# A rewritten order list for a fused attention and gated MLP kernel: four operations change their places in the queues, and two things derived from the list change with it

## The chip, the cores and the metric

The kernel runs on one core of a Trainium2 chip. A time is the device time of one launch in microseconds (us); of several runs the median is given. The core has TensorE (PE: matmuls, and PEld for its weight loads), VectorE (DVE), ScalarE (ACT), GpSimd (POOL), and SyncE (SP), whose queue issues the DMA transfers.

## The reference

```python
def _attn_ref(q, k, v):                       # (4, 12, 448, 64) each
    scores = (1 / np.sqrt(64)) * np.matmul(q, k.transpose(0, 1, 3, 2))
    scores = np.where(mask, -1e9, scores)     # mask: above the diagonal
    scores = scores - np.max(scores, axis=-1, keepdims=True)
    attn = np.exp(scores)
    attn = attn / (np.sum(attn, axis=-1, keepdims=True) + 1e-09)
    return np.matmul(attn, v)

def _moe_ref(x, w_in, w_spatial, b_spatial, w_out):
    h = np.maximum(x @ w_in, 0.0)             # x: (4, 448, 768), the heads side by side
    u, v = h[..., :512], h[..., 512:]
    v_n = (v - mean(v)) / np.sqrt(var(v) + 1e-06)
    v_s = np.einsum('ts,bsd->btd', w_spatial, v_n) + b_spatial[None, :, None]
    return (u * v_s) @ w_out                  # (4, 448, 768)
```

## The kernel before

The work is written as a plan of 2496 operations, numbered in the order in which the functions of the kernel add them. An operation (`plan.add`) is one or a few instructions of one engine, with the tiles that it reads and writes. The heads are taken in 24 pairs (`p`; four batches of six pairs), and each batch goes through the gated MLP (`ffn`) once its pairs are done.

- `load(p)` (L701, L708) fetches q and k of a pair; the early pairs in four loads of 112 KB, one per head. `v_load` (L876) fetches v, `prep_in` (L1324) a piece of `w_in`.
- `qk_turn(p)` turns q and k with transposes on PE (L738, L764) and copies them out of PSUM (L747, L749, L785, L787); for the later pairs a DMA transpose does it and DVE or POOL copies it `across` (L847).
- `wide(p)` serves the early pairs: scores (L934), row maximum on DVE (L972), exponential on ACT (L982), sums (L993, L1001), scaling (L487 to L491), PE transposes (L1021), copies (L1045, L1047). `attend(p)` serves the others: scores (L1101, L1102), mask and maximum (L1112), exponential (L1124), weights (L1213), and for all pairs the product with v (L1255). `gram` (L583) and `total` (L604) are PE work for scale factors.
- `ffn(b)` has, for each of four tiles of rows (`t`, 128 rows and at the end 64), a chain of matmuls (L1473) into a PSUM bank `pf`, ReLU on ACT into a buffer `hv` (L1536), statistics (L1544 to L1570, with a power on POOL at L1563), the normalisation (L1580, L1582, L487) and the low half of the result into `vn` (L1595, on DVE or POOL). Then follow `u`, the product with `w_spatial`, and the output. `hv` has two buffers for the four tiles.

Engines are set by a string `WHERE`, and the order by hand, in the list `ORDER` (from L57), one sequence of all 2496 numbers. `Plan.run` (L237) walks the list once and puts each operation at the end of its engine's queue. So only the order of two operations of one engine reaches the chip. But two more things are taken from the walk.

*Buffers.* A buffer is given to an operation's tile at the tile's first use in the list, from the front of a line of free ones, and returns to the end of that line at its last use in the list. The operation then waits for all that used the buffer before:

```python
if b.slot is None:
    b.slot, b.before = free[b.kind].pop(0)
    left[b] = len(b.ops)
waits += b.before
```

*Fillers.* The walk keeps a clock of its own for every engine (`busy`), made of costs written in the source. DVE work and POOL work that stand next to each other in the list exclude each other in this clock (`pool_end`, `dve_end`). While the clock of PE is under `WARM = 46000` (ns), and PE would have to wait for the next operation by this clock, it puts filler matmuls into PE's queue, `self.warm` (L689: ones times ones, 128 x 128 by 256 columns of f16, into PSUM bank 2 of `pf`, read by nobody):

```python
while now + (fill := FILL if now > 6000 else 2 * FILL) < start - 40:
    order.append((self.warm, e))
    now += fill
```

The clock is used for nothing else: at run time the filler stands in PE's queue as any matmul.

Of the kernel before, what the change touches and what calls it, by code (L numbers as in the profile page):

```python
# [56 lines left out]
    10, 1, 5, 0, 3, 73, 8, 6, 72, 100, 2, 75, 74, 4, 9, 14, 12, 11, 15, 96, 13, 26, 97, 22, 98, 93, 7, 16, 148, 18,  # L57
    17, 92, 99, 149, 20, 19, 95, 101, 21, 102, 106, 107, 103, 110, 108, 111, 104, 109, 76, 114, 113, 105, 116, 112,
    115, 27, 120, 118, 117, 157, 28, 119, 94, 121, 164, 126, 132, 160, 158, 165, 127, 122, 161, 166, 78, 23, 167,
    123, 168, 162, 79, 139, 159, 163, 124, 170, 136, 169, 77, 125, 172, 142, 137, 171, 256, 138, 131, 173, 140, 176,  # L60
    29, 152, 141, 143, 177, 257, 153, 30, 190, 128, 193, 150, 174, 133, 178, 24, 154, 151, 130, 129, 144, 175, 156,
    155, 194, 181, 135, 134, 25, 261, 195, 186, 179, 185, 34, 180, 191, 260, 196, 264, 80, 187, 265, 192, 84, 82,
    268, 188, 31, 189, 83, 267, 269, 262, 266, 32, 270, 197, 272, 271, 274, 263, 273, 33, 275, 258, 276, 38, 198,
    182, 81, 35, 259, 46, 278, 36, 184, 277, 315, 279, 280, 37, 183, 316, 318, 285, 42, 282, 253, 283, 284, 319,
    145, 314, 290, 281, 252, 328, 321, 294, 306, 322, 320, 326, 300, 297, 307, 323, 329, 254, 39, 317, 255, 325, 40,
    327, 295, 330, 85, 296, 41, 324, 298, 289, 86, 286, 43, 331, 503, 301, 44, 287, 397, 291, 288, 332, 302, 87, 45,
    202, 310, 88, 334, 402, 47, 333, 311, 89, 500, 338, 90, 336, 335, 146, 206, 351, 398, 48, 293, 147, 344, 348,
    309, 49, 312, 339, 50, 395, 51, 199, 52, 399, 308, 60, 57, 299, 394, 63, 66, 313, 58, 61, 292, 403, 200, 59, 54,
    502, 404, 201, 64, 396, 55, 337, 62, 406, 303, 414, 354, 416, 415, 56, 410, 67, 407, 411, 417, 405, 343, 510,
    409, 207, 412, 572, 208, 501, 413, 509, 203, 587, 69, 422, 423, 507, 418, 573, 304, 439, 588, 419, 204, 408,  # L70
    440, 209, 349, 441, 420, 520, 210, 421, 305, 350, 427, 522, 497, 521, 340, 65, 523, 426, 355, 342, 431, 53, 345,
    341, 356, 352, 424, 205, 400, 70, 428, 425, 346, 524, 68, 214, 401, 589, 347, 498, 353, 429, 506, 496, 430, 525,
    71, 508, 505, 526, 499, 532, 528, 436, 504, 725, 533, 357, 442, 529, 534, 538, 531, 432, 536, 535, 956, 211,
    539, 212, 443, 530, 437, 358, 542, 213, 433, 537, 574, 543, 215, 222, 444, 435, 549, 527, 359, 434, 438, 544,
    216, 734, 511, 91, 545, 540, 513, 445, 561, 737, 548, 541, 738, 558, 512, 741, 217, 739, 562, 546, 742, 554,
    218, 559, 563, 547, 514, 553, 590, 560, 446, 564, 729, 570, 740, 447, 733, 731, 730, 555, 223, 1030, 732, 591,
    557, 743, 224, 728, 550, 556, 744, 726, 565, 225, 552, 515, 727, 566, 551, 735, 1029, 516, 1052, 517, 518, 519,
    955, 567, 751, 219, 907, 745, 977, 747, 746, 752, 220, 748, 736, 908, 1293, 753, 757, 788, 749, 568, 221, 226,
    750, 569, 783, 1292, 785, 754, 795, 784, 770, 791, 592, 781, 796, 786, 762, 755, 227, 792, 779, 763, 593, 756,
    780, 787, 758, 798, 789, 228, 782, 773, 594, 793, 1033, 797, 229, 767, 799, 575, 794, 1031, 230, 800, 231, 771,  # L80
    232, 805, 234, 764, 237, 759, 246, 602, 240, 235, 247, 238, 236, 617, 576, 241, 239, 243, 603, 242, 249, 577,
    806, 244, 362, 801, 363, 817, 604, 248, 360, 595, 766, 760, 361, 802, 364, 765, 618, 365, 761, 807, 250, 790,
    245, 772, 251, 816, 774, 370, 596, 808, 835, 368, 366, 978, 367, 837, 369, 1032, 605, 775, 597, 834, 371, 836,
    811, 606, 812, 833, 838, 818, 373, 824, 813, 598, 819, 820, 768, 599, 372, 803, 607, 769, 839, 600, 374, 814,
    375, 578, 815, 840, 821, 376, 804, 377, 378, 579, 383, 822, 387, 809, 847, 619, 381, 843, 385, 848, 620, 776,
    384, 887, 389, 823, 388, 849, 382, 1051, 850, 386, 841, 777, 810, 580, 390, 844, 641, 827, 888, 778, 825, 601,
    846, 642, 581, 851, 845, 1034, 889, 826, 233, 853, 828, 582, 608, 857, 890, 379, 391, 891, 1053, 583, 852, 893,
    894, 842, 895, 584, 892, 609, 829, 854, 896, 1054, 901, 910, 610, 1058, 1059, 855, 898, 392, 830, 917, 902,
    1055, 393, 856, 611, 903, 448, 899, 460, 913, 585, 612, 858, 911, 1057, 918, 831, 900, 613, 859, 861, 914, 643,
    614, 1060, 921, 644, 586, 904, 919, 862, 860, 832, 615, 655, 920, 616, 621, 915, 622, 864, 449, 876, 656, 869,  # L90
    450, 1291, 623, 877, 1065, 1294, 624, 645, 451, 916, 868, 1290, 646, 625, 879, 452, 870, 1295, 873, 1056, 453,
    626, 657, 1299, 380, 872, 878, 1301, 627, 905, 897, 658, 923, 922, 628, 906, 874, 571, 863, 461, 659, 924, 454,
    629, 462, 1066, 912, 1062, 630, 463, 865, 875, 1067, 484, 871, 660, 866, 1063, 929, 880, 867, 631, 925, 1064,
    980, 632, 927, 661, 992, 926, 633, 930, 634, 1068, 981, 993, 943, 982, 635, 647, 648, 455, 946, 931, 456, 886,
    636, 881, 928, 457, 464, 1004, 994, 939, 983, 1016, 490, 458, 465, 1005, 882, 995, 985, 1061, 1017, 984, 459,
    1069, 932, 996, 997, 986, 1006, 1070, 1018, 987, 998, 485, 637, 999, 1041, 486, 988, 1000, 638, 989, 1300, 487,
    1001, 639, 990, 1306, 466, 1019, 991, 488, 1039, 669, 979, 1007, 909, 1020, 491, 885, 670, 1003, 1021, 489, 944,
    1296, 1002, 933, 671, 1022, 1008, 949, 945, 672, 1010, 1009, 1024, 492, 640, 947, 950, 1011, 934, 493, 662, 948,
    467, 478, 938, 1012, 649, 468, 1013, 940, 1297, 1367, 469, 663, 1015, 883, 472, 470, 1014, 1315, 942, 1303, 951,
    884, 1023, 935, 471, 1304, 1316, 1327, 941, 1307, 1317, 1339, 1305, 937, 673, 494, 664, 1366, 1340, 650, 1308,  # L100
    1298, 1328, 1318, 1368, 1341, 665, 1319, 1369, 1329, 683, 495, 1342, 1370, 666, 684, 1309, 936, 1330, 1320,
    1314, 674, 1321, 1351, 1343, 1332, 1373, 1371, 473, 952, 1331, 1352, 675, 1377, 1322, 1365, 1333, 1374, 1345,
    1344, 1334, 1324, 479, 474, 1380, 685, 480, 1040, 1323, 1353, 1346, 475, 676, 1025, 481, 1335, 677, 1336, 1378,
    678, 1381, 1325, 1038, 1379, 1338, 651, 1348, 1364, 1354, 1337, 1347, 652, 1355, 1326, 953, 1382, 679, 1356,
    954, 653, 1310, 667, 1357, 1383, 1026, 668, 1349, 654, 1350, 958, 1311, 1358, 686, 1027, 680, 482, 1401, 957,
    476, 1028, 1389, 681, 483, 687, 959, 1042, 1413, 960, 961, 964, 682, 962, 1302, 697, 968, 965, 1390, 1414, 698,
    971, 1388, 969, 1415, 708, 1123, 972, 970, 709, 1360, 688, 973, 1425, 1416, 703, 1391, 689, 1035, 974, 699,
    1426, 1417, 704, 477, 966, 1392, 1419, 1418, 1402, 710, 1393, 1124, 1359, 1420, 1403, 700, 1384, 1421, 1394,
    1395, 1422, 711, 701, 1441, 705, 1396, 1424, 1397, 706, 1423, 1440, 1663, 692, 1398, 1439, 975, 693, 976, 1037,
    1664, 963, 1399, 1442, 967, 707, 1400, 1662, 1086, 712, 1098, 1404, 1087, 713, 1044, 694, 1088, 1665, 714, 1099,  # L110
    1089, 1443, 695, 1444, 1438, 1100, 1090, 1140, 1091, 1445, 1447, 1512, 1101, 1451, 1092, 1448, 1093, 715, 1094,
    1385, 1103, 696, 1095, 1452, 716, 1102, 1096, 717, 1453, 1097, 1036, 1104, 1372, 1446, 1110, 1105, 1107, 1454,
    1141, 1111, 1106, 1043, 1142, 1108, 1455, 1112, 1109, 1456, 1406, 1045, 1074, 1405, 1113, 1114, 719, 1075, 1115,
    1073, 1457, 1076, 1046, 1143, 1047, 1077, 1048, 1116, 720, 1078, 1049, 721, 1079, 1119, 1071, 1080, 722, 1081,
# [1646 lines left out]
```

## Time and profile before

| | |
|---|---|
| median of 3 runs | 358.98 us (358.64, 358.98, 359.28) |
| span of the profiled execution | 358.6 us |
| PE busy | 346.2 us, 97% |
| PEld busy | 225.5 us, 63% |
| DVE busy | 285.9 us, 80% |
| ACT busy | 268.7 us, 75% |
| POOL busy | 161.6 us, 45% |
| mean granted TensorE clock | 0.998 of full speed |

The span runs from the first to the last instruction of the one profiled execution; the time of a run holds what lies around that too. For the profiled execution the page gives the span alone. A timeline row is a run of like instructions: its start, its length from the first start to the last end, how many, and the idle time of the engine before it with what ended that. Ends of matmuls are modelled: rows that follow each other on PE overlap.

### The profile page before, as it was taken

How to read it: one execution, taken by the hardware profiler on the slowest of the kernel's cores; microseconds unless marked ns; L12 is line 12 of the kernel's file. 1: busy time of each engine (PE TensorE's matmuls, PEld its weight loads, DVE VectorE, ACT ScalarE, POOL GpSimd, SP SyncE). 2: the span in 40 equal slices, each digit the busy share in tenths (PEclk: the TensorE clock that was granted, in tenths of full speed). 3: DMA queues.
4: the chain of work that ended last, by engine and by line, in shares of the span. 5: the costliest groups of instructions: out<-in, count | busy, mean ns of one | idle time of the engine just before them, and what ended most of it. 6: DMA issues, size and time to landing. Idle time of an engine off the chain costs nothing.

```text
span 358.6 us, 8098 instructions
## 1 busy us (share of the span) xinstructions
PE 346.2 (97%) x2602; PEld 225.5 (63%) x2602; DVE 285.9 (80%) x1116; ACT 268.7 (75%) x767; POOL 161.6 (45%) x223
## 2 busy tenths in 40 slices
PE   6999899999999999999999999999999999999995
PEld 5476555665555556765455579755755885555695
DVE  4899889999999999889898998987989994263420
ACT  3698899999999999888799989748789684231101
POOL 3133664337656468364374572334686710042400
PEclk9999999999999999999999999999999999999999
DMA  7959979746768999999997898997767978300014
GB/s 162 210 164 242 244 170 215 174 100 166 150 166 186 208 237 181 178 182 139 188 180 153 172 225 162 205 174 156 164 116 156 159 111 174 82 2 0 3 47 130
DMA packets 160796, 55.84 MB, mean 156 GB/s; under 512 B 155249, under 2 KB 156530, under 8 KB 160754
## 3 DMA queue, kind: packets, MB, share of 16 engines
q1 hardware_dynamic: 160754, 55.33, 74.5%
q8 instruction: 20, 0.33, 0.4%
q14 instruction: 22, 0.18, 0.1%
HBM read 26.76 MB, written 5.51 MB: 90 GB/s over the span
## 4 chain that ended last, share of the span: by engine, by line
PE 65%; DMA 10%; DVE 8%; ACT 7%; POOL 4%; issue 3%; SPq 2%; POOLq 0%; ACTq 0%; DVEq 0%
PE pf L1473 43%; PE px L1255 6%; DMA qkT<-qks 4%; PE ps L1021 3%; PE ps L934 3%; PE ps L1101 3%; ACT e L982 3%; PE ps L1102 2%; DMA et<-e 2%; PE ps L764 2%; POOL qks L523 2%; DVE ps L972 1%; DMA o<-in_moe_w_out_dram 1%; DMA wst<-wb 1%; ACT e L489 1%
## 5 line engine op out<-in xcount | busy, mean ns | idle before, releaser
L1473 PE MATMUL pf<-wi,xT 128*128 128x512 f16 (+1 forms) x360 | 61.6, 338 | 0.0
L1473 PE MATMUL pf<-xT,wi 128*128 128x448 f16 x288 | 59.3, 353 | 0.4 <-ACT hv L1536 0.4
L1124 ACT ACTIVATE ps<-ps,sm 128x384 f32<-128x384 f32 (+4 forms) x98 | 45.4, 463 | 13.2 <-DVE sm L1112 8.0
L1473 PE MATMUL pf<-wo,g 128*128 128x384 f32 x288 | 54.9, 341 | 0.0
L1213 DVE SCALAR_TENSOR_TENSOR e<-ps,sm,e 128x256 f16<-128x256 f32 (+4 forms) x98 | 46.3, 505 | 6.3 <-ACT e L489 6.3
L1473 PEld LDWEIGHTS pf<-wo,g 128*128 128x128 f32 x288 | 49.8, 188 | 2.0 <-issue 1.1
L489 ACT ACTIVATE e<-ps,sm 128x256 f16<-128x256 f32 (+4 forms) x98 | 44.3, 509 | 5.5 <-DVE sm L1146 1.9
L1112 DVE CUSTOM_DVE_ANT_0 ps<-ps,mask,sc 128x256 f32<-128x256 f32 (+4 forms) x98 | 47.2, 506 | 1.4 <-PE ps L1102 0.8
L1473 PEld LDWEIGHTS <-wi 128*128 128x128 f16 x288 | 27.4, 98 | 26.7 <-issue 3.0
L1473 PEld LDWEIGHTS <-xT 128*128 128x128 f16 (+1 forms) x360 | 27.2, 103 | 25.4 <-issue 4.7
L491 POOL TENSOR_SCALAR e<-e,sm 128x384 f32<-128x384 f32 (+3 forms) x43 | 23.8, 566 | 41.5 <-ACT e L982 13.6
L982 ACT ACTIVATE e<-ps,sm 128x256 f32<-128x256 f32 (+3 forms) x70 | 34.3, 500 | 4.6 <-DVE sm L972 2.6
L1473 PE MATMUL pf<-wst,vn 128*128 128x448 f16 (+1 forms) x176 | 36.0, 353 | 0.1
L523 POOL TENSOR_TENSOR qks<-qk,qks 112x512 f16<-112x512 f32 x21 | 24.2, 1157 | 20.3 <-ACT qks L489 8.9
L934 PE MATMUL ps<-qkT 64*128 64x128 f32 (+3 forms) x160 | 28.5, 444 | 0.9 <-ACT e L982 0.7
L1102 PE MATMUL ps<-qkT 128*64 128x256 f16 (+4 forms) x196 | 26.3, 284 | 0.4 <-DVE qkT L847 0.4
L1473 PEld LDWEIGHTS <-vn 128*128 128x128 f16 (+1 forms) x176 | 16.8, 98 | 15.2 <-issue 0.5
L1101 PE MATMUL ps<-qkT 128*64 128x256 f16 (+4 forms) x196 | 24.8, 291 | 0.9 <-DVE e L1213 0.7
L972 DVE CUSTOM_DVE_ANT_0 ps<-ps,e 128x128 f32<-128x128 f32 (+2 forms) x60 | 24.3, 441 | 1.2 <-PE ps L934 1.0
L1021 PE MATMUL ps<-ident,e 128*128 128x128 f32 x160 | 23.8, 279 | 1.3 <-POOL e L491 0.5
L1563 POOL TENSOR_TENSOR ln<-ln,mhalf 128x1 f32<-128x1 f32 (+1 forms) x16 | 10.6, 666 | 31.5 <-DVE ln L1555 26.8
L1021 PEld LDWEIGHTS ps<-ident,e 128*128 128x128 f32 x160 | 17.6, 141 | 9.1 <-issue 3.3
(168 smaller groups left out, 729.5 us busy)
## 6 DMA issues: line engine op xcount, KB each, us to landing
wb<-in_moe_w_in_dram SPq DMA_DIRECT2D x12, 512.0 KB, 4.3
vnat<-in_v_dram SPq DMA_DIRECT2D x24, 192.0 KB, 3.9
out_dram<-o SPq DMA_DIRECT2D x12, 384.0 KB, 3.0
qk<-in_k_dram SPq DMA_DIRECT2D x14, 224.0 KB, 4.0
qk<-in_q_dram SPq DMA_DIRECT2D x14, 224.0 KB, 4.2
o<-in_moe_w_out_dram SPq DMA_DIRECT2D x8, 384.0 KB, 4.1
qk<-in_q_dram SPq DMA_DIRECT2D x20, 112.0 KB, 4.8
qk<-in_k_dram SPq DMA_DIRECT2D x20, 112.0 KB, 3.6
```

The source lines that it names most:

```text
L489: nc.scalar.activation(out=dst, in_=src, func=AF.Copy, scale=scale)
L523: lambda e: HANDLE[e].tensor_tensor(out=dst_l(), in0=src(), in1=dst_h(), op=ALU.subtract),
L934: nc.tensor.matmul(out=at(bank)[r0:r0 + rn, o0:o0 + n], lhsT=flat32(t)[rows, q0:q0 + rn], rhs=k32(t)[rows, :n], start=True, stop=True, ski ...
L972: lambda e, ps=ps, n=n, u=u0 + u, sm=sm, o0=o0, h=h: nc.vector.tensor_tensor_reduce(out=at(ps)[:, o0:o0 + n], in0=at(ps)[:, o0:o0 + n], in ...
L982: lambda e, ps=ps, n=n, u=u0 + u, sm=sm, o0=o0, c=c: nc.scalar.activation(out=at(eb)[:, 128 * c:128 * c + n], in_=at(ps)[:, o0:o0 + n], fu ...
L1021: nc.tensor.transpose(out=at(pt)[:, 128 * i:128 * i + 128], in_=e32(at(eb))[:, c0 + i, :], identity=ident)
L1101: nc.tensor.matmul(out=o, lhsT=w, rhs=qkT[:, 2 + x, :n], start=True, stop=False)
L1102: nc.tensor.matmul(out=o, lhsT=w, rhs=qkT[:, 4 + x, :n], start=False, stop=True)
L1112: lambda e, ps=ps, n=n, u=u, sm=sm, o0=o0, m0=m0: nc.vector.tensor_tensor_reduce(out=at(ps)[:, o0:o0 + n], in0=at(ps)[:, o0:o0 + n], in1=m ...
L1124: nc.scalar.activation(out=dst, in_=src, func=AF.Exp, scale=-1.0, bias=at(sm)[:, u:u + 1], accum_out=at(sm)[:, 4 + 2 * u:5 + 2 * u],)
L1213: lambda e, part=part, src=src, sm=sm, u=u: nc.vector.scalar_tensor_tensor(out=part(1), in0=src(), scalar=at(sm)[:, 12 + u:13 + u], in1=pa ...
L1473: nc.tensor.matmul(out=o, lhsT=a(), rhs=rhs, start=(n0 + n == 0), stop=(n0 + n == len(mms) - 1), skip_group_check=len(out_ap()) > 1,)
```

## The change

The list `ORDER` is written anew in a total order that differs almost everywhere; `WHERE`, the functions and all costs stay. The lines of the diff with the numbers that matter here:

```diff
--- before.py
+++ after.py
@@ -54,133 +54,134 @@
...
-    123, 168, 162, 79, 139, 159, 163, 124, 170, 136, 169, 77, 125, 172, 142, 137, 171, 256, 138, 131, 173, 140, 176,
-    29, 152, 141, 143, 177, 257, 153, 30, 190, 128, 193, 150, 174, 133, 178, 24, 154, 151, 130, 129, 144, 175, 156,
...
-    145, 314, 290, 281, 252, 328, 321, 294, 306, 322, 320, 326, 300, 297, 307, 323, 329, 254, 39, 317, 255, 325, 40,
...
-    1055, 393, 856, 611, 903, 448, 899, 460, 913, 585, 612, 858, 911, 1057, 918, 831, 900, 613, 859, 861, 914, 643,
...
-    1069, 932, 996, 997, 986, 1006, 1070, 1018, 987, 998, 485, 637, 999, 1041, 486, 988, 1000, 638, 989, 1300, 487,
...
-    1395, 1422, 711, 701, 1441, 705, 1396, 1424, 1397, 706, 1423, 1440, 1663, 692, 1398, 1439, 975, 693, 976, 1037,
...
-    2378, 2339, 2379, 2371, 2340, 2341, 2412, 2413, 2372, 2342, 2414, 2343, 2415, 2416, 2373, 2350, 2417, 2351,
...
+    127, 162, 139, 163, 255, 168, 124, 136, 137, 170, 169, 94, 171, 256, 78, 125, 172, 79, 77, 138, 173, 140, 176,
+    152, 29, 141, 142, 257, 177, 193, 143, 128, 131, 133, 190, 130, 153, 30, 174, 150, 156, 129, 178, 144, 135, 24,
...
+    856, 910, 830, 917, 1055, 392, 393, 448, 899, 611, 903, 913, 585, 858, 831, 612, 613, 614, 1057, 460, 918, 919,
...
+    988, 1000, 989, 990, 1001, 1300, 1019, 466, 488, 1306, 1039, 637, 638, 1007, 639, 885, 979, 991, 1020, 1021,
...
+    1440, 1423, 963, 1398, 1399, 1037, 967, 1400, 1664, 692, 693, 707, 1442, 712, 1662, 713, 1404, 975, 1044, 976,
...
+    2339, 2340, 2341, 2342, 2371, 2372, 2373, 2350, 2351, 2352, 2353, 2414, 2415, 2416, 2417, 2398, 2399, 2400,
+    2343, 2418, 2381, 2354, 2391, 2401, 2392, 2393, 2394, 2355, 2356, 2380, 2382, 2383, 2419, 2402, 2357, 2384,
```

Split up by engine, the old and the new list give the same queues on PE, ACT and POOL (fillers aside), and these differences:

```
SP    load of pair 4, k, second head (255): from behind 254 to ahead of 94 (k of pair 2), 78, 79, 77 (v);
      the 19 issues from 94 to 254 stand one place later
DVE   613 (L1570, MLP of batch 0, t=2): ahead of 1057 (L551) and 918 (L972) instead of behind
DVE   1300 (L545, scale of pair 13): behind 487 (L1301) and 990 (L1213) instead of ahead
DVE   975, 976 (L847, across of pair 11): behind 963 (L551), 1399 (L1213), 967 (L810), 1400 (L1213)
      instead of ahead
```

The two things that are taken from the walk, worked through on both lists:

```
fillers, in all          before 32, after 58
  ahead of PE operation  137  143  194  261  197  263  298  291   47   49  303
  before                   1    0    2    1    0    2    0    1    0    1    0
  after                    4    8    0    4    8    1    1    2    2    1    3
  (24 further ones, up to operation 159, are the same)
hv of batch 3, t=1 (2350, L1536): before the buffer of t=0, whose last user is 2343 (L1595, POOL);
      after that of t=2, whose last user is 2373 (L1595, DVE)
hv of batch 2, t=1 (1777, L1536): in the same way 1770 (L1595, DVE) before, 1800 (L1595, POOL) after
```

Here 137, 143, 194 and 197 are transposes of `wide` (L1021), 261 and 263 scores of pair 3 (L934), 298, 291 and 47 PE work of about 33 to 38 us, 49 the `total` (L604) ahead of the transposes of pair 4's k (312, L764), and 303 a piece behind those. Some PSUM banks (`ps`), `vn`, `g` and `ln` buffers change names too.

## Rows read from the trace of the kernel before

**Rows 1.** Page: busy time by engine; clock granted to TensorE in 40 slices.
```profile
PE 346.2 (97%) x2602; PEld 225.5 (63%) x2602; DVE 285.9 (80%) x1116; ACT 268.7 (75%) x767; POOL 161.6 (45%) x223
...
PEclk9999999999999999999999999999999999999999
```
**Rows 2.** Page: the chain of work that ended last, by engine.
```profile
PE 65%; DMA 10%; DVE 8%; ACT 7%; POOL 4%; issue 3%; SPq 2%; POOLq 0%; ACTq 0%; DVEq 0%
```
**Rows 3.** Windows: stretch, its length, busy us by engine, clock, DMA share, GB/s.
```profile
16.00:24.00 8.00, 7.80 (x62) 5.52 (x61) 7.18 (x31) 7.38 (x26) 4.14 (x8) 1.00 0.53 142
24.00:40.00 16.00, 14.93 (x138) 10.29 (x136) 15.24 (x62) 14.07 (x48) 4.75 (x9) 1.00 1.02 239
```
**Rows 4.** Timeline of PE, 38 to 40.2 us: pair 4's transposes and their wait.
```profile
38.19 0.38 PE L604 MATMUL pf<-wacc,ones 128*128 128x1 f32 x2
39.58 0.57 PE L764 MATMUL ps<-ident,qk 112*128 112x112 f32 x4 [1.01 <-DMA qk<-in_k_dram]
```
**Rows 5.** Timeline of SP: DMA issues; start, length, line, count.
```profile
13.11 0.76 SPq L701 DMA_DIRECT2D qk<-in_k_dram  x1
13.90 1.94 SPq L876 DMA_DIRECT2D vnat<-in_v_dram  x3
...
32.68 2.00 SPq L701 DMA_DIRECT2D qk<-in_k_dram  x2
```
**Rows 6.** DMA view of 32.65 to 33.2 us: one issue, KB, us to landing.
```profile
qk<-in_k_dram SPq DMA_DIRECT2D x1, 112.0 KB, 4.9
```
**Rows 7.** DMA view of 12.9 to 13.6 us, the same columns.
```profile
qk<-in_k_dram SPq DMA_DIRECT2D x1, 112.0 KB, 3.4
```
**Rows 8.** Timeline of PE, 16 to 27 us: fillers and the operations that follow.
```profile
16.24 0.94 PE L689 MATMUL pf<-ones 128*128 128x256 f16 x7
...
19.56 0.60 PE L764 MATMUL ps<-ident,qk 112*128 112x112 f32 x4
20.00 1.33 PE L1021 MATMUL ps<-ident,e 128*128 128x128 f32 x10
21.17 0.55 PE L764 MATMUL ps<-ident,qk 112*128 112x112 f32 x4
...
22.53 0.93 PE L934 MATMUL ps<-qkT 64*128 64x128 f32 x8 [0.15 <-DVE qkT L787]
...
24.10 0.85 PE L583 MATMUL pf<-vnat 128*128 128x128 bf16 x12
...
26.32 0.38 PE L689 MATMUL pf<-ones 128*128 128x256 f16 x2
26.63 0.97 PE L934 MATMUL ps<-qkT 64*64 64x448 f32 x4
```
**Rows 9.** Timeline of DVE, 27 to 28 us: the maximum behind that last score.
```profile
27.75 0.63 DVE L972 CUSTOM_DVE_ANT_0 ps<-ps,mask 128x448 f32<-128x448 f32 x1 [0.23 <-ACT e L982]
```
**Rows 10.** Chain of waits, 312 to 330 us: start, length, piece.
```profile
317.55 1.16 POOL vn L1595
...
318.74 0.70 ACT hv L1536
...
319.48 10.57 PE pf L1473 x55
```
**Rows 11.** Timeline of DVE, 315 to 322 us: 2373, the low half of t=2.
```profile
317.56 1.69 DVE L1595 TENSOR_TENSOR vn<-hv,vn 128x512 f16<-128x512 f32 x1
```
**Rows 12.** Timeline of DVE, 146 to 153 us: the copies across, the weights.
```profile
149.28 0.79 DVE L847 COPY qkT<-qkT 64x896 f16<-64x896 f16 x2 [1.08 <-DMA qkT<-qks]
...
150.48 0.61 DVE L1213 SCALAR_TENSOR_TENSOR e<-ps,sm,e 128x384 f16<-128x384 f32 x1
```
**Rows 13.** Timeline of PE, 149 to 152 us: the scores behind these.
```profile
151.14 0.30 PE L1101 MATMUL ps<-qkT 128*64 128x256 f16 x2 [0.34 <-DVE e L1213]
```

**Rows 14.** Timeline of DVE, 116 to 119.5 us: 487, which 1300 now follows.
```profile
117.68 0.56 DVE L1301 SCALAR_TENSOR_TENSOR hv<-o,hv 128x384 int32<-128x384 int32 x1
```
**Rows 15.** Timeline of POOL, 116 to 119.5 us: 1306, which waits for 1300.
```profile
117.81 0.99 POOL L491 TENSOR_SCALAR qk<-qk,sc 112x512 f32<-112x512 f32 x1 [1.24 <-DVE sc L545]
```

241 rows, old and new, of the table ORDER are left out of this document.

## The prediction

> **What bounds the kernel now.** I read the busy times first: PE has work for 346.2 of 358.6 us, and every digit of its granted clock is a 9, so there is little idle time to win and no clock to win [rows 1]. The chain that ended last agrees: PE holds 65% of it, no other engine over 10% [rows 2]. The question is therefore where PE is idle, or where something more is put into its queue. The windows show that only the start and the end have slack: PE works 7.80 of 8 us from 16 to 24, and 14.93 of 16 from 24 to 40, where DVE is as full, 15.24 of 16 [rows 3]. The timeline of PE then shows that of the 1.07 idle us of the second stretch 1.01 lie in one place, at 39.58, where the transposes of pair 4's k wait for its load [rows 4]. Near the end the chain shows one wait that is not PE's own: the buffer of L1595, then ReLU L1536, then a row of 55 matmuls without a gap [rows 10].
>
> **The change part by part.** Of the queues, only those of SP and DVE change. But the list also decides where fillers stand and who waits for which buffer, and I price these with the moves.
>
> *The load of pair 4 (255).* It was the second of two issues that take 2.00 us from 32.68 [rows 5], and PE waited 1.01 us for it [rows 4]. After the change it goes out near 13.1, some 20 us before its use. What is late next is the other half, 254: issued at 32.68, landing after 4.9 us at 37.58 [rows 6], while PE without the wait reaches the transposes at 39.58 - 1.01 = 38.57. That leaves 1.0 us of cover, so the whole wait goes: -1.0, with bounds 0 (254 or a neighbour lands late instead) and -1.0. In front, the move puts one issue of 0.76 us ahead of 94 and of three v loads [rows 5]. 94 would go out at 13.9 and land 3.4 us later [rows 7], about 17.3, for transposes at 21.17; the v issues would end at 15.84 + 0.76 = 16.6, and with the same flight (an estimate from the nearest load) land by 20.0 for the gram work at 24.10 [rows 8]. Transfers take 0.53 of the DMA engines in 16 to 24 us [rows 3], so there is room. Cost 0; were the cover gone, it is 0.76. All 19 issues up to 254 keep their order, and those behind 254 can only go out earlier.
>
> *The fillers.* There are 26 more. One takes (0.94 - 0.38) / (7 - 2) = 0.11 us of PE [rows 8], so at most 2.9 us, at least 0 if each falls into a wait. I go through them in order. Three more ahead of 137 and eight ahead of 143, the first of the ten transposes at 20.00: that row and the transposes of 19.56 ahead of it overlap, with no idle time noted [rows 8]. PE is not waiting there, so the 11 push everything back, 11 x 0.11 = 1.2. Two fewer ahead of 194: -0.2, so 1.0. Three more ahead of 261: it waited for a DVE copy, 0.15 us [rows 8], and that copy follows the transposes of 21.17, now 1.0 later themselves, so the wait moves along; with the one filler that stood there it holds some 0.3 us. I take these three at 0. Eight more ahead of 197 and one fewer ahead of 263: 7 x 0.11 = 0.8. The two old ones at 26.32 stand there for a wait [rows 8]; I take it as real and let it swallow 0.2, so 0.6. At 263 PE is then 1.6 to 1.7 late. Does this pass on? 263 ends at 26.63 + 0.97 = 27.60, and DVE starts the maximum behind it at 27.75 after 0.23 us of idling [rows 9]. The row names ACT as releaser, but the operand is 263's. So DVE becomes late by as much, and at 15.24 of 16 us busy [rows 3] it cannot make it good before 40. The last seven (ahead of 298, 291, 47 and 303) stand where PE is behind DVE and ACT, which are now late as well: 0 to 0.8, I take 0.1. Sum +1.8, bounds 0 and +2.9. Had the load stayed, its 1.0 us of wait would have swallowed part of this; with the load moved both terms stand.
>
> For the low end of this term a rule of the Trainium skill speaks (Perfetto Trace Analysis, section "Identifying the Most-Contended Engine"): matmul busy time is no good measure of how near TensorE is to its limit, since pipelined matmuls look otherwise in a trace, and the busy share of weight loads is a better one. By that share, 10.29 of 16 us, PE would have a third of the stretch free and the fillers could cost nothing; by the matmul rows they cost what stands above. I go by the rows, because a filler's place is in a queue that runs in order, and the rows show 0.11 us from one to the next.
>
> *The buffer `hv` in the last batch.* L1536 at 318.74 (2350) follows the end of POOL's L1595, 317.55 + 1.16 = 318.71, and the matmuls at 319.48 follow it at once [rows 10]. In the new list its buffer comes from tile 2, whose last user is DVE's L1595: 317.56 + 1.69 = 319.25 [rows 11]. So ReLU starts 0.54 later, and the 55 matmuls behind it, which have no gap, too: +0.54, bounds 0 (if the gaps of the last 28 us take it back) and +0.6. The like swap in batch 2 (1777) waits for 1800 instead of 1770; I find no reader that is near its limit there and put it at 0, with bounds 0 and +0.54 by the same rows.
>
> *The three DVE moves.* 975 and 976 wait 1.08 us for a DMA transpose [rows 12]; four small operations now go ahead of them. The last of these, 0.61 long, has kept PE waiting 0.34 at 151.14 [rows 13]. It could run in the idle time, a gain of up to 0.3, or run past 149.28 and hold up the copies and PE by up to 0.6. 1300 goes behind an operation of 0.56 us [rows 14] and one of L1213, at most 0.61 [rows 12]; POOL's L491 at 117.81 waits for it [rows 15], so POOL is late by up to 1.2 us, but POOL is busy for 45% of the span only [rows 1]: 0, bounds 0 and +0.6. 613 passes two operations; the longer is a maximum, at most 0.63 [rows 9]: bounds -0.3 and +0.3, value 0. Together I take +0.1, with -0.6 and +1.5 at the far ends. Renamed PSUM banks and the other buffers: 0, for the order on PE is the same.
>
> Sum: -1.0 + 1.8 + 0.54 + 0.1 = +1.44. The profiled execution spans 358.56 us, 0.42 less than the median of 358.98; I add the sum to the median: 360.4 us.
>
> **The rivals.**
>
> *Fillers hidden, the load's gain stays: faster.* If PE was waiting at all the places where the planner's clock says so, all 26 fillers fall into waits, and -1.0 is what is left; if the ReLU of the last batch is hidden as well, the time is 358.0, with that cost in it 358.98 - 1.0 + 0.54 = 358.5. It decides at 20.00: if that row starts within 0.3 us of where it was in spite of eleven fillers ahead, this case holds. For it: PE's ends are modelled, and short waits can be hidden in rows that overlap. Against it: the rows from 19.56 to 21.17 leave no room for 1.2 us. This is also where the rule above leads.
>
> *The load brings nothing.* 254, or a neighbouring transfer at 24 to 40 us, where the DMA engines are busy at 1.02 of their time [rows 3], lands late and PE waits as before. Then 360.4 + 1.0 = 361.4. Against it: 1.0 us of cover at 254, and PE comes later, not earlier.
>
> *The early load pushes others.* The 0.76 us of one issue comes out at PE from 16 to 25 us, through pair 2's k or v: 360.4 + 0.76 = 361.2. Against it: 3.9 and 4.1 us of cover.
>
> *The change is nothing.* The load's wait and the fillers meet in one place: the first 1.0 us of late PE is paid by the wait that goes, the rest by waits behind it, and the tail hides the 0.54. Then 359.0.
>
> **How the numbers follow.** A measurement of this kernel can tell about 0.2% from no change, 0.72 us: from 358.26 to 359.70 is the same. Chances: the forecast 0.55, of which 0.05 comes out under 359.70; the load brings nothing 0.12; the early load pushes 0.03; fillers hidden with the tail paid 0.15 (same), with the tail hidden 0.10 (faster); nothing 0.05 (same). Slower: 0.50 + 0.12 + 0.03 = 0.65; same: 0.05 + 0.15 + 0.05 = 0.25; faster 0.10. The range reaches down over the cases of hidden fillers to 358.2 and up to 361.8, which takes in the late load (361.4) and half of the filler bound (2.9 - 1.8 = 1.1). The forecast's own range is 359.6 to 361.5.
>
> **What would show it.** Right: 58 records of L689 instead of 32; the ten transposes of 20.00 start 1.0 to 1.3 later; the maximum of 27.75 some 1.6 later; no DMA wait ahead of pair 4's transposes, which start at about 40.2; near the end ReLU L1536 released by DVE's L1595, and the 55 matmuls start 0.54 later after it than they otherwise would. Wrong: the ten transposes near 20.0 with all fillers in place; a new wait of L764 or L583 for a load at 17 to 25 us; a DMA wait at 39 to 41 us; or a shift between 40 and 310 us that these steps don't hold.

## The result

The changed kernel takes 363.64 us (median of 4 runs, 363.14 to 363.89), the kernel before 358.93 (358.64 to 359.28) beside it. The ratio is 1.0133, with a 95% interval of 1.0119 to 1.0147: 4.7 us slower. Forecast was 360.4, with 361.8 as the upper end: the direction was right, the size was not, by 3.2 us.

The page of the changed kernel, busy time and granted clock, answers to [rows 1]:

```profile
PE 348.0 (96%) x2628; PEld 227.2 (63%) x2628; DVE 286.5 (79%) x1116; ACT 268.8 (74%) x767; POOL 161.3 (45%) x223
...
PEclk9999999999999999999999999999999999999999
```

There are 26 more matmuls and 26 more weight loads (2628 against 2602), and 1.8 us more PE work, in a time 4.7 us longer. The row of the granted clock is the same as before. The windows, with the columns of [rows 3]:

```profile
16.00:24.00 8.00, 7.95 (x67) 5.89 (x65) 6.22 (x24) 6.93 (x23) 3.77 (x7) 1.00 0.59 143
24.00:40.00 16.00, 16.00 (x151) 11.48 (x149) 14.42 (x61) 13.47 (x46) 4.29 (x9) 1.00 0.98 230
```

In the stretch of the fillers PE has no idle time left, while DVE fell from 15.24 to 14.42 of 16 us: PE holds up DVE there now, as the maximum of [rows 9] shows, which waited 0.23 us before (timeline of DVE):

```profile
28.66 0.63 DVE L973 CUSTOM_DVE_ANT_0 ps<-ps,mask 128x448 f32<-128x448 f32 x1 [0.90 <-PE ps L935]
```

The timeline of PE shows the added fillers (L690, one line further down than before) and what follows them, as in [rows 4, 8]:

```profile
17.29 0.61 PE L690 MATMUL pf<-ones 128*128 128x256 f16 x4
...
19.39 1.04 PE L690 MATMUL pf<-ones 128*128 128x256 f16 x8
20.26 1.25 PE L1022 MATMUL ps<-ident,e 128*128 128x128 f32 x10
...
26.02 1.05 PE L690 MATMUL pf<-ones 128*128 128x256 f16 x8
...
27.54 0.97 PE L935 MATMUL ps<-qkT 64*64 64x448 f32 x4
...
39.57 0.58 PE L765 MATMUL ps<-ident,qk 112*128 112x112 f32 x4
```

In this execution PE was 0.85 us ahead at 16.4 us (the scores in front of these fillers start at 16.38, before at 17.23). It came to its full pace sooner: four like transposes still take 0.95 us at 7.92 in the kernel before, and 0.55 at 7.53 in the changed one (timelines of PE, first before, then after):

```profile
7.92 0.95 PE L738 MATMUL ps<-ident,qk 112*128 112x112 f32 x4
```

```profile
7.53 0.55 PE L739 MATMUL ps<-ident,qk 112*128 112x112 f32 x4
```

The windows view gives both stretches a granted clock of 1.00, so why is not shown. It does not come from the change: the first scores start at 9.69 before, at 8.85 in the changed kernel, and also at 8.66 in `b_load` and 9.72 in `b_613` (both below). Against that head start the ten transposes are 0.85 + 0.26 = 1.1 late, the last score 0.85 + 0.91 = 1.76, and pair 4's transposes 0.84, with no wait for the load any more. So far it is as forecast: 1.0 to 1.3, 1.6, and 1.8 - 1.0.

The rest of the loss comes later, which is the forecast's own sign of being wrong: a shift between 40 and 310 us that its steps don't hold. The timeline of DVE at 120 us and of ACT at 137 us, each with a new wait for a transfer, and that of PE behind the second:

```profile
120.61 1.01 DVE L1291 TENSOR_SCALAR hv<-o 128x384 int32<-128x384 int32 x1 [1.07 <-DMA o<-in_moe_w_out_dram]
```

```profile
136.72 0.63 ACT L490 ACTIVATE qks<-qk 112x512 f16<-112x512 f32 x1 [0.93 <-DMA qkT<-qks]
```

```profile
139.39 1.62 PE L1256 MATMUL px<-et,vs 128*64 128x448 f16 x24 [1.11 <-DVE xT L1278]
```

At the end of the chain, as in [rows 10], ReLU now follows DVE's L1596, as forecast:

```profile
320.02 1.70 DVE vn L1596
...
321.81 0.70 ACT hv L1537
...
322.54 9.62 PE pf L1474 x50
```

One more term was put at nothing in the forecast and costs something: the renamed PSUM banks. In the kernel before the transposes at 52 us follow each other, in the changed one the second group waits (timeline of PE, first before, then after):

```profile
52.62 0.56 PE L764 MATMUL ps<-ident,qk 112*128 112x112 f32 x4
53.02 0.49 PE L1021 MATMUL ps<-ident,e 128*128 128x128 f32 x3
```

```profile
52.84 0.59 PE L765 MATMUL ps<-ident,qk 112*128 112x112 f32 x4
53.61 0.55 PE L1022 MATMUL ps<-ident,e 128*128 128x128 f32 x3 [0.17 <-ACT et L1046]
```

From one group to the next it is 0.40 before and 0.77 after.

A word on the profiles: wherever a run gives both, the device time is 1.7 to 2.1 us above the span (363.6 and 361.6 here). The profiled execution of the kernel before, with 358.6, was therefore a long one, of 360.3 to 360.7, and not 0.42 under the median as the forecast had it. Runs of the kernel before, unchanged, lie between 357.2 and 361.0 in all.

### The profile page after: what moved, and what is told of

It is laid out like the page before. It is cut to its first block, busy times and chain, and to the rows that moved or that the text cites. A ratio compares the mean times of both kernels' runs of the same rounds, so it can differ in the third digit from the quotient of the medians.

```text
span 361.6 us, 8148 instructions
## 1 busy us (share of the span) xinstructions
PE 348.0 (96%) x2628; PEld 227.2 (63%) x2628; DVE 286.5 (79%) x1116; ACT 268.8 (74%) x767; POOL 161.3 (45%) x223
## 4 chain that ended last, share of the span: by engine, by line
PE 48%; ACT 4%; DMA 2%; DVE 2%; issue 1%; SPq 1%; POOL 0%; ACTq 0%; POOLq 0%
PE pf L1474 39%; PE px L1256 4%; PE ps L1102 3%; PE ps L1103 2%; DMA et<-e 1%; ACT junk L568 1%; ACT e L490 1%; DMA out_dram<-o 1%; ACT ps L1125 1%; DVE e L1214 1%; SPq L1230 1%; DVE vn L1596 0%; ACT hv L1537 0%; ACT o L1685 0%; POOL ln L1564 0%
## 5 line engine op out<-in xcount | busy, mean ns | idle before, releaser
L935 PE MATMUL ps<-qkT 64*128 64x256 f32 (+3 forms) x160 | 28.3, 444 | 0.7 <-ACT e L983 0.7
```

Source lines behind the costliest of these rows:

```text
L935: nc.tensor.matmul(out=at(bank)[r0:r0 + rn, o0:o0 + n], lhsT=flat32(t)[rows, q0:q0 + rn], rhs=k32(t)[rows, :n], start=True, stop=True, ski ...
```

## The experiments

Every kernel was timed in five rounds beside the kernel before. In them the fillers are fixed by a table, so that a change in the list doesn't move them. In the rows shown, line numbers are 2 lower than before (L1288 for L1290), or 3 higher where a second kind of filler is added (L1293). Differences in us are those of the medians. The fillers' table stands in place of the walk's clock:

```diff
-                if busy[e] < WARM and (2, []) in free["pf"]:
-                    now = max(...)
-                    while now + (fill := ...) < start - 40: ...
+                order += [(self.warm, e)] * FILLERS.get(n, 0)
```

### The fillers alone, the change without them, and the load alone

`b_fill58` has the table `137:4, 143:8, 261:4, 197:8, ...` of the changed list in the kernel before. `a_fill32` is the changed kernel with the old table. `b_load` moves one number:

```diff
-    ... 329, 254, 39, 317, 255, 325, ...
+    ... 329, 254, 39, 317, 325, ...
-    ... 28, 119, 94, ...
+    ... 28, 119, 255, 94, ...
```

`b_code26` keeps the 32 fillers and adds 26 matmuls of 8 columns in the places of the new ones:

```diff
+                order += [(self.small, e)] * SMALL.get(n, 0)
+        plan.small.fn = lambda e: nc.tensor.matmul(out=phys["pf"][2][:, 0:8], lhsT=half[:, 0:128], rhs=half[:, 0:8], ...)
```

> The kernel before, its order, buffers and loads untouched, with the 58 fillers of the changed kernel in their places instead of 32. Theory 1 (the fillers and the 52 more instructions of PE that they bring are the cause; where PE's code is fetched moves, and a fetch on the DMA engines makes transfers late that PE waits for, at 117 to 121 and 133 to 137 us of the changed kernel): 358.9 + 1.8 of PE time - 1.0 that the wait for pair 4's load swallows + 1 to 2.5 of late transfers: 360.7 to 362.5. Theory 2 (the three DVE moves cost the 2.3 us of the middle): 359.7, the PE time of the fillers alone.

> The kernel before with its 32 fillers and 26 further matmuls of 8 columns in the places of the added fillers: as many more instructions in PE's stream as the changed kernel has, but each of some 0.03 to 0.06 us instead of 0.11. Theory 1: half to all of what the full fillers cost beyond their own time remains, 359.9 to 362. Theory 2: at most 26 x 0.06 = 1.6 of PE time, of which 1.0 falls into the wait for pair 4's load: 358.9 to 359.5.

> The changed kernel with the 32 fillers of the kernel before in their places; all its moves and buffers stay. Theory 1: load -1.0, buffer hv +0.54, DVE moves about +0.1: 358.6, within 0.7. Theory 2: 358.9 - 1.0 + 0.54 + 2.3 = 360.7 or more.

> The kernel before with the one move of the load (255 ahead of 94), 32 fillers, all else as before. Both theories: the wait of 1.01 us ahead of pair 4's transposes goes, 357.9; if another transfer is late instead, 358.9.

Before: 358.72. `b_fill58` 362.12 (ratio 1.0106, 1.0086 to 1.0125), `b_code26` 360.15 (1.0041, 1.0022 to 1.0060), `a_fill32` 361.38 (1.0079, 1.0060 to 1.0098), `b_load` 358.23 (0.9986, 0.9969 to 1.0003). So the fillers cost 3.4, not 1.8, as theory 1 has it; `b_code26`, with 1.4, lies in its range too, and above that of theory 2. But the rest of the change costs 2.7 without any added filler, as theory 2 has it: neither is the whole. From `a_fill32` to the changed kernel it is 2.3 more. The two parts, 3.4 and 2.7, make 6.1, more than the 4.7 of both together. They meet in one place: at 118 us DVE loses time in `a_fill32` too, though not by a late load (timeline of DVE; the next section shows why):

```profile
118.25 2.17 DVE L1288 TENSOR_SCALAR hv<-o 128x384 int32<-128x384 int32 x1
```

The load is worth 0.5, and the interval holds zero; mostly there is no wait to take away. Of the eleven traces with this load in its old place, eight show at most 0.2 us of wait ahead of pair 4's transposes of k, and three 0.68 to 1.01. This is the timeline of PE in `b_613` (below), one of the eight:

```profile
38.48 0.58 PE L762 MATMUL ps<-ident,qk 112*128 112x112 f32 x4
```

### The move of 1300, undone and alone; 613; the buffers

`b_1300` and `b_613` move one number each in the kernel before, `a_1300` moves one back in the changed kernel:

```diff
 b_1300  -  989, 1300, 487, 1001, 639, 990, 1306,
         +  989, 487, 1001, 639, 990, 1300, 1306,
 a_1300  -  ... 999, 459, 486, 487, ... 989, 990, 1001, 1300, 1019,
         +  ... 999, 459, 486, 1300, 487, ... 989, 990, 1001, 1019,
 b_613   -  911, 1057, 918, 831, 900, 613,
         +  911, 613, 1057, 918, 831, 900,
```

> The kernel before with the one move of 1300 behind 487 and 990; fillers, loads and buffers as before. Theory A (POOL starts 1306 some 1.2 us later, has no gap left, and DVE's conversion L1290 of 384 elements, 0.34 us long elsewhere, stands still until POOL is done, 2.17 us in the run of the changed kernel with 32 fillers; PE waits for the transposes behind it): 358.7 + 1.2 to 1.8 = 359.9 to 360.5, L1290 at about 117 to 120 us with 1 to 2.2 us. Theory B (the loss at 117 to 123 us comes from late transfers, not from this move): 358.7, L1290 with 0.34 us.

> The changed kernel with 1300 back ahead of 487 and 990; its 58 fillers and all else stay. Theory A: 363.6 - 1.2 to 1.8 = 361.8 to 362.4. Theory B: 363.6.

> The kernel before with the one move of 613 ahead of 1057 and 918. Theory A: within 0.3 of before, 358.7. Theory B (this move holds up the maximum behind it, and with it PE near 102 us): 359.0 to 359.3.

Before: 358.66. `b_1300` 360.51 (1.0049, 1.0031 to 1.0067), `a_1300` 363.46 (1.0141, 1.0122 to 1.0161; the changed kernel has 1.0133), `b_613` 358.79 (1.0005, 0.9989 to 1.0020). So 1300 alone costs 1.85, and undoing it in the changed kernel brings nothing: theory A is right in one kernel and theory B in the other. The timelines tell why. DVE and then POOL in `b_1300`:

```profile
118.35 2.16 DVE L1288 TENSOR_SCALAR hv<-o 128x384 int32<-128x384 int32 x1
120.43 0.60 DVE L1211 SCALAR_TENSOR_TENSOR e<-ps,sm,e 128x384 f16<-128x384 f32 x1
```

```profile
117.87 0.69 POOL L489 TENSOR_SCALAR qk<-qk,sc 112x512 f32<-112x512 f32 x1 [2.03 <-DVE sm L1136]
118.50 0.20 POOL L1069 MEMSET e<- 128x128 f16 x1
118.68 1.00 POOL L1452 TENSOR_TENSOR wo<-hv,wo 128x384 fp32r<-128x384 f32 x1
119.66 0.64 POOL L489 TENSOR_SCALAR e<-e,sm 128x448 f32<-128x448 f32 x1
```

The same stretch in `b_load`, where 1300 stands ahead:

```profile
117.45 0.34 DVE L1288 TENSOR_SCALAR hv<-o 128x384 int32<-128x384 int32 x1
```

```profile
116.24 0.99 POOL L489 TENSOR_SCALAR qk<-qk,sc 112x512 f32<-112x512 f32 x1 [1.23 <-DVE sc L543]
117.17 0.20 POOL L1069 MEMSET e<- 128x128 f16 x1
117.53 1.12 POOL L1452 TENSOR_TENSOR wo<-hv,wo 128x384 fp32r<-128x384 f32 x1 [0.16 <-ACT wo L487]
```

There POOL ends the small operation at 117.37 and starts the next at 117.53, and DVE's conversion slips into that gap with 0.34 us. With 1300 late POOL starts 0.48 us ahead of the conversion instead of 1.21, and has no gap until 120.30; the conversion comes to DVE at 118.35 and ends at 120.51, 0.2 behind POOL. Everything behind it on DVE waits. The Trainium skill (SBUF — State Buffer, section "SBUF: two separate sides") says that VectorE, in some of its modes or with two inputs in SBUF, and GpSimd share a pair of ports that one of them holds for a whole instruction while the other stands still. The trace agrees that the conversion stands still beside POOL, 2.16 against 0.34 us for one and the same operation; but it stands through four POOL operations in a row, not one, and no run shows in which mode it ran.

In `a_1300` the gap is there again, but the conversion's data is not. The timeline of DVE:

```profile
120.52 0.74 DVE L1288 TENSOR_SCALAR hv<-o 128x384 int32<-128x384 int32 x1 [1.08 <-POOL wo L1452]
```

It starts as late as in the changed kernel (120.61). The row names POOL's L1452, which ends at 120.43; but the load, issued at 114.74, takes 5.7 us and lands at the same moment, and in `b_code26` the like conversion starts at 119.23, before that POOL operation ends there at 119.31. So POOL is not what it needs. The views of DMA issues show why (one issue, KB, us to landing): first the kernel before, then the changed one, then `b_code26w` (below).

```profile
o<-in_moe_w_out_dram SPq DMA_DIRECT2D x1, 384.0 KB, 4.5
```

```profile
o<-in_moe_w_out_dram SPq DMA_DIRECT2D x1, 384.0 KB, 5.7
```

```profile
o<-in_moe_w_out_dram SPq DMA_DIRECT2D x1, 384.0 KB, 5.6
```

The load of `w_out` lands 1.1 to 1.2 us later in its flight. In all six traces with longer code (the changed kernel, `a_1300`, `b_fill58` and the three `b_code` kernels) this flight takes 5.1 to 5.7 us, in the ten others 3.8 to 4.6. Either cause makes DVE late at this place, so taking away one of them brings nothing.

The buffers: `a_buf2` is the changed list with all four moves undone and 32 fillers, so that only PSUM banks, `hv`, `vn`, `g` and `ln` differ from the kernel before; `b_hv` puts 2343 behind 2350 in the old list, which swaps the last batch's `hv` and nothing else; `b_975` puts 975 and 976 behind 1400.

> The changed kernel's buffers alone: all queues and the 32 fillers as before, but PSUM banks, hv, vn, g and ln as the new list gives them. Theory A (hv costs its 0.54, PSUM banks nothing): 358.7 + 0.54 = 359.2. Theory B (the renamed PSUM banks cost the 0.9 us that the changed kernel with 32 fillers loses between 40 and 102 us against the kernel with the moved load): 360.1.

> The kernel before with the one swap of hv in the last batch: ReLU 2350 takes the buffer of tile 2 and waits for DVE's L1595. The step as forecast: 358.7 + 0.54 = 359.2, ReLU L1536 released by DVE's L1595 and 0.5 later after it than before. If the gaps of the last 28 us take it back: 358.7.

> The kernel before with the one move of 975 and 976 behind four small DVE operations. As forecast: within 0.3 of before. Rival (they run past the landing of the DMA transpose and hold up PE): 358.7 + 0.6 = 359.3.

Before: 358.72. `b_hv` 359.18 (1.0019, 1.0006 to 1.0033), +0.46 for the 0.54 of the forecast. `a_buf2` 360.03 (1.0041, 1.0024 to 1.0059), 0.85 above `b_hv`: theory B is nearer, and the wait at 53 us shown above is part of it. `b_975` 358.97 (1.0005, 0.9985 to 1.0026): too little to tell by the time. Its trace shows the rival at work all the same (timeline of PE):

```profile
149.14 0.24 PE L1100 MATMUL ps<-qkT 128*64 128x192 f16 x1 [1.06 <-DVE qkT L845]
```

In `b_613`, without this move, PE waits 0.41 for this copy and 0.34 a little later. From the small product in front (L602, at 147.60 and 148.11) to the scores at 154.53 and 154.59 it is 6.93 us in `b_975` and 6.48 in `b_613`: 0.45 more. The changed kernel waits the same 1.06, at 153.20.

### The place of PE's code

`b_code39` adds 13 small matmuls ahead of operation 105 to the 26 of `b_code26`. `b_code26w` puts all 26 ahead of 105, where PE waits:

```diff
 b_code39   +SMALL = {137: 3, 143: 8, 261: 3, 197: 8, 298: 1, 47: 2, 303: 1, 105: 13}
 b_code26w  +SMALL = {105: 26}
```

> The kernel before with 39 matmuls of 8 columns instead of 26: the 26 in the places of the added fillers, and 13 more ahead of the scores at 12.7 us, which wait there. Each brings two instructions. With 26, the code fetch that comes at 123.0 in the kernel before came at 114.7, where the last piece of a load of w_out landed 2.0 us behind its first, and DVE waited 0.91 for it. Theory 1 (it is where the fetch falls): with 13 more it comes some 3.5 us earlier still, near 111, the load of w_out is whole before DVE asks for it, and most of the 1.4 us goes: 358.7 to 359.5. Rival (each further instruction costs by itself, 26 cost 1.4): 358.7 + 2.1 = 360.8.

> The kernel before with 26 matmuls of 8 columns all ahead of the scores at 12.7 us, where PE waits 0.68 us: at 0.026 us each (8 of them took 0.21 in the run with 26) they fit into that wait, and from 44 us on PE's code lies where it lies in the changed kernel. Theory 1 (where PE's code is fetched matters by itself): the fetch comes at about 115, the load of w_out is late as in the run with 26, 358.7 + 0.7 to 1.0 = 359.4 to 359.7. Rival (the 26 cost 1.4 by their own time on PE): 358.7.

`b_code39` took 360.61 (1.0064, 1.0045 to 1.0082, before 358.72): the forecast of theory 1 failed and the rival's 360.8 fits. `b_code26w` took 360.53 (1.0060, 1.0042 to 1.0079, before 358.27): +2.3, and here the rival fails, since the 26 cost PE nothing; theory 1's 359.4 to 359.7 is too low as well. The timeline of PE in `b_code26w`:

```profile
9.32 2.38 PE L937 MATMUL ps<-qkT 64*128 64x128 f32 x12
11.63 0.81 PE L692 MATMUL pf<-ones 128*128 128x8 f16 x26
12.37 0.97 PE L937 MATMUL ps<-qkT 64*64 64x448 f32 x4
```

From the end of one group of scores to the next it is 12.37 - 9.32 - 2.38 = 0.67, as in the kernel before. What is longer is PE's code, by 52 instructions. The code comes in pieces of 16 KB (q8 in the DMA view, 20 pieces before, 21 after; q14, which also brings code, has 22 in both). The DMA view of 122.8 to 123.6 us of the kernel before shows one, and that of 115.8 to 116.6 us of the changed kernel another:

```profile
q8 instruction: 1, 0.02, 9.1%
```

```profile
q8 instruction: 1, 0.02, 8.6%
```

In the kernel before the two pieces of this stretch come at 123.0 and 138.4, in the changed kernel at 116.0 and 133.7. In `b_code26w` they come at 115.4 and 132.2, in `b_code39` at 112.2 and 131.3. In all six traces with longer code transfers of these two stretches are late: the load of `w_out` above, and the transpose issued near 130, with 5.4 to 5.7 us against 4.2 to 4.4 in the ten others (first the kernel before, then the changed one):

```profile
qkT<-qks SPq DMA_TRANSPOSE x1, 4.3
```

```profile
qkT<-qks SPq DMA_TRANSPOSE x1, 5.7
```

In `b_code26w` DVE and ACT wait as in the changed kernel:

```profile
120.00 0.40 DVE L1293 TENSOR_SCALAR hv<-o 128x384 int32<-128x384 int32 x1 [0.98 <-DMA o<-in_moe_w_out_dram]
```

```profile
135.31 0.63 ACT L488 ACTIVATE qks<-qk 112x512 f16<-112x512 f32 x1 [0.72 <-DMA qkT<-qks]
```

The Trainium skill (Runtime: NRT & Kernel Launch, section "Instruction fetch mechanics") says that an engine's code is refilled in blocks of 16 KB, 256 instructions, by a DMA queue of its own, and that this is mostly hidden. The 16 KB agree. Whether the refill is hidden here is open: 52 instructions that cost PE nothing cost 2.3 us.

That a fetch makes a transfer late was not tried by itself. What is shown is that longer code alone costs this much, and that the late transfers and the moved fetches come together. At the transpose ACT waits 0.72 to 0.96 us in all six traces with longer code, and in none of the ten others; in each of the six a piece of q8 comes between its issue and its landing, in none of the ten. At the load of `w_out` DVE waits 0.69 to 1.07 in five of the six, in `a_1300` the 1.08 above, and in none of the ten. In `b_code39` the fetch at 112.2 lies 1.5 us ahead of the issue of `w_out`, and DVE still waits 0.69. But it falls into the flight of the load of k that is issued in front, at 112.19, and that load is late too (DMA views, first the kernel before, then `b_code39`):

```profile
qk<-in_k_dram SPq DMA_DIRECT2D x1, 224.0 KB, 4.5
```

```profile
qk<-in_k_dram SPq DMA_DIRECT2D x1, 224.0 KB, 5.5
```

A transfer can be late without a fetch as well: the next load of `w_out`, issued at 118.26, takes 4.4 us in the kernel before and 3.6 in `b_load`. DVE waits 0.67 for it in the kernel before, at 122.77, though the fetch comes only at 123.0.

### The conversion moved, and fewer fillers

`b_1300_491` is `b_1300` with operation 491, the conversion that stood still, behind 1022. `b_load_f24` is `b_load` without the 8 fillers behind operation 159.

```diff
 b_1300_491  -  ..., 491, ..., 1003, ..., 1296, 1002, ..., 1022, ...
             +  ..., 1003, ..., 1296, 1002, ..., 1022, 491, ...
```

> The kernel with the move of 1300, and DVE's conversion 491 (L1290, the one that stood 2.16 us) moved behind the next four DVE operations, so that it comes to DVE at about 119.9 and not at 118.3, while POOL is busy from 117.9 to 120.3 as there. Theory (the conversion stands still while POOL works, and everything behind it on DVE with it): the weights L1213 ahead of it run at once, L1290 takes under 1 us, and most of the 1.8 goes: 358.8 to 359.3. Rival (late POOL work itself costs, through 1306): 360.5.

> The kernel with the moved load and 24 fillers: the 8 behind operation 159 are left out, the place where the added ones stand. If the old ones cost PE time there as the added ones do: 8 x 0.11 = 0.9 at most less, 357.4 to 358.0; if they stand in real waits: 358.2. PE's code is 16 instructions shorter, which moves the fetches a little later; a late load from that is the rival that would make it slower.

Before: 358.27. `b_1300_491` took 358.89 (1.0020, 1.0005 to 1.0035): of 1.85 some 0.6 is left. The conversion takes 0.50, and the weights L1211 start behind the reciprocal at once (timeline of DVE):

```profile
117.46 0.60 DVE L1211 SCALAR_TENSOR_TENSOR e<-ps,sm,e 128x384 f16<-128x384 f32 x1
...
119.12 0.50 DVE L1288 TENSOR_SCALAR hv<-o 128x384 int32<-128x384 int32 x1
```

POOL is as late and as dense as in `b_1300`, so it is the standing still that costs. `b_load_f24` took 359.01 (1.0017, 1.0000 to 1.0033), 0.7 above the kernel before, where `b_load` was 0.5 below it: the 8 old fillers cost PE no time that comes back, they fill waits, and the shorter code did not help. No kernel here beats the one before beyond its interval; `b_load` comes nearest.

## Why the forecast was wrong

- *The load.* Forecast -1.0, measured -0.5 (-1.1 to +0.1). The mechanism is right, and nothing behind the load became late; but the wait of [rows 4] is not one that every execution has. The rival in which the early load pushes others did not come: pair 2's transposes and the gram work show no wait for a load.
- *The fillers: the step that failed.* "Sum +1.8, bounds 0 and +2.9." The delay on PE came out as worked through: 1.1 at the ten transposes, 1.76 at the last score, passed on by DVE (the terms of that sum make 1.7 to 1.8). But the fillers alone cost 3.4 (`b_fill58`), above the upper bound, since the sum counted their time on PE and put their 52 instructions at nothing. As many instructions cost 1.4 in the same places with 0.03 us each (`b_code26`), and 2.3 without time on PE (`b_code26w`). The loss stands where transfers are late, near 120 and 135 us; how longer code makes them late is not proven.
- *The hv buffer.* Forecast +0.54, measured +0.46. Right. The PSUM banks, "0, for the order on PE is the same", cost 0.85 together with the small buffers: the same order on PE doesn't keep a bank free as early.
- *The DVE moves: the second step that failed.* 1300 was put at 0 with a bound of +0.6 "since POOL is busy for 45% of the span only"; alone it costs 1.85. A mean over the span said nothing of the next 2 us of POOL, and the operation that lost was not the one that waited for 1300 but one on DVE. In the changed kernel this cost does not show, for the late load has the same effect at the same place: there either step alone would have been enough to miss. 613 cost nothing, as forecast. 975 with 976 cost 0.25 by the time, within its interval, and 0.45 by PE's rows; the forecast had 0.6 for the case that they hold up the copies, and did not take it.
- *The sum.* The measured parts: -0.5 + 3.4 + 0.46 + 0.85 + 0.1 + 0.25, and nothing for 1300 beside the late load, are 4.6; measured 4.7. Each part is good to half a us or a little more, so that they meet this closely is luck. The order counts as well: with the other parts in place the fillers are worth 2.3, inside the forecast's bounds, and the rest alone 2.7 where the forecast had -0.4.

## What to carry to other kernels

Added instructions can have a second price beside their time: they make the engine's code longer, which moves the moments at which it is fetched. Here a change at 20 us is paid at 120 and 135 us, where transfers land later; that the fetches are the link is likely and not proven. A test with as many instructions that take no time tells the two apart. When an edit moves work on GpSimd, ask which VectorE operations now stand beside it, not only who waits for it; and when undoing a suspect brings nothing, put it alone into the kernel before, since two causes may hide each other.

## What was not expected of the hardware

- One VectorE operation of 128x384 int32 took 0.34, 0.50 or 2.16 us, depending on what GpSimd did beside it.
- 52 more instructions of TensorE without time on the engine made the program 2.3 us longer (1.5 to 2.8).
- TensorE's like rows got shorter at different moments in executions of like kernels (four transposes 0.95 us at 7.92 in one, 0.55 at 7.53 in another, both at a granted clock of 1.00 by the view), and the first scores started at 8.6 to 9.8 us. That is about one us of difference between profiles with nothing behind it in the code.
